# A fused LayerNorm, S5 state space and GLU kernel: the first block set by hand, weight pair 0 on two DMA rings ahead of x tiles 2 and 3

## The chip, the core and the metric

The kernel runs on one core of a Trainium2 chip. The metric is the device time of one execution in microseconds (us); medians are over several executions, and before and after were run in turn on the same chip. An execution counts as slow when it is more than 1.5% above the fastest of its kernel.

Below, TensorE is PE in the profile, its weight loads PEld, VectorE DVE, ScalarE ACT, GpSimd POOL, SyncE SP. Times in traces are from the start of the core's span, which is about 1.8 us shorter than the device time. A profiled run is one execution, so its details can differ from the median's.

## The reference

```python
xn = layernorm(x)                       # x: 2048 tokens of 576
h[t] = Lam_bar * h[t-1] + B_bar @ xn[t] # 576 complex states
y = 2 * real(C @ h) + xn * Dskip
g, u = xn @ w_gate, xn @ w_up           # 576 to 4608
out = x + y + (sigmoid(g) * u) @ w_down # 4608 to 576, bf16 out
```

Most of the time is in the three large products of the last line. The tokens are worked in blocks of 512 (four tiles of 128), two blocks at a time, and the 4608 hidden columns in 36 chunks of 128. For TensorE the kernel transposes the normalised x: xT holds, for a block, the 576 features over partitions.

## The kernel before, as far as the argument goes

The kernel writes the work of all engines in one order, and a queue of background work (`bg`) is dealt out to DVE and ScalarE between groups of matmuls. Loads, in program order (in the trace of the kernel before, what SyncE issues moves on queue q1, 29808 packets, and what ScalarE issues on q10, 432 packets, both listed as hardware; GpSimd's is on q0, 12672 packets, listed as software; a ring is such a queue below):

```python
for tt in range(TT_B):                          # x tiles 0..3, 144 KB each, rows of 1152 bytes
    load_x(tt, nc.sync if tt % 2 == 0 else nc.scalar)
for pr in range(2):                             # weight pairs 0, 1: 576 KB each, rows of 512 bytes
    load_wgu((0, pr), nc.gpsimd, nc.gpsimd)
for tt in range(TT_B, 2 * TT_B):                # x tiles 4..7 (block 1)
    load_x(tt, nc.gpsimd, "hst")
for pr in range(2, 4):
    load_wgu((0, pr), nc.gpsimd, nc.gpsimd)
# ... Dskip
load_wgu((0, 4), nc.gpsimd, nc.gpsimd)
```

A weight pair holds the gate and up columns of two chunks. One gate/up group is 18 matmuls of 64 rows and 512 columns. Groups 0 and 1 are begun by hand on the first two tiles while tiles 2 and 3 are still being normalised; then come groups 2 to 9 of block 0, and then groups of block 1, whose xT comes by four DMA transposes that SyncE issues:

```python
busy(10, TB); busy(6, P)                        # dummy matmuls
for tt in range(2):
    ln_stats(tt); ln_std(0, tt, tt + 1)
for tt in range(2):
    ln_recip(0, tt, tt + 1); ln_norm(tt, twice=False)
    start_transpose(tt)                         # TensorE
busy(20, P)
start_copy(0, slice(0, NH), nc.scalar.copy)     # PSUM to xT
ln_stats(2)
start_copy(1, slice(0, 5), nc.scalar.copy)
# ... statistics of tile 3, rest of copy 1 on DVE, norms of tiles 2 and 3
start_groups[0].mms(slice(0, 2 * P))            # 18 matmuls of 256 columns
start_transpose(2); start_transpose(3)
start_groups[1].mms(slice(0, 2 * P))
# ... copies of tiles 2 and 3
for g in start_groups:
    g.mms(slice(2 * P, TB))
for tt in range(TT_B, 2 * TT_B):                # block 1's LayerNorm: background work
    bg.add(1.05, lambda tt=tt: ln_stats(tt))
# ... std, norms, ln_dma_transpose(4..7), 8 residuals, then
bg.add(1.0, exp_first, ready=lambda: consts_at[0] is not None and consts_at[0] + 4 <= bg.now)
```

`exp_first` makes tables for the state space part from nine small constant loads (`load_consts`), which are issued among the groups of block 1.

Of the kernel before, what the change touches and what calls it, by code (L numbers as in the profile page):

```python
# [66 lines left out]
def kernel(  # L67
# [65 lines left out]

    def load_x(tt, eng, tag=None):
        if tag is None:
            xt = lnp.tile([P, D], BF16, name="xt", bufs=8)
        else:
            xt = hpool.tile([P, D], BF16, name="xt0", tag=tag, bufs=10)
        eng.dma_start(xt[:], x[tt * P:(tt + 1) * P, :])
        xts[tt] = xt  # L140
# [23 lines left out]
    make_identity(nc, ident[:])  # L164
    for tt in range(TT_B):
        load_x(tt, nc.sync if tt % 2 == 0 else nc.scalar)
    for pr in range(2):
        load_wgu((0, pr), nc.gpsimd, nc.gpsimd)
    for tt in range(TT_B, 2 * TT_B):
        load_x(tt, nc.gpsimd, "hst")  # L170
    for pr in range(2, 4):
        load_wgu((0, pr), nc.gpsimd, nc.gpsimd)
    dskip_rows = consts.tile([P, D], BF16, name="dskip_rows")
    nc.gpsimd.dma_start(dskip_rows[:], A_Dskip.partition_broadcast(P))
    load_wgu((0, 4), nc.gpsimd, nc.gpsimd)

# [12 lines left out]
    ldt = consts.tile([P, NU], FP32, name="ldt")  # L189
    consts_at = [None]  # L190

    def load_consts():
        for (dst, src) in ((ldt, A_log_dt), (lre, A_Lambda_re), (lim, A_Lambda_im)):
            nc.gpsimd.dma_start(dst[:, 0:PT], src[0:R0].rearrange("(a p) -> p a", p=P))
            for h0 in (0, H):
                nc.gpsimd.dma_start(dst[h0:h0 + H, PT:NU], src[R0:NS].rearrange("(a b) -> a b", b=1))
        consts_at[0] = bg.now

# [284 lines left out]
    class GateUp:  # L483
# [5 lines left out]

        def mms(self, cols=slice(0, TB)):  # L490
            w = wgu_t[(self.slot, self.f // FP)]
            fs = slice((self.f % FP) * P, (self.f % FP + 1) * P)
            for c in range(NH):
                for gi, rows in ((0, slice(0, H)), (1, slice(H, P))):
                    nc.tensor.matmul(self.ps[:, gi, cols], w[rows, c, fs], xT[self.nb][rows, c, cols],  # L495
                                     start=c == 0, stop=c == NH - 1)
# [65 lines left out]
    def d_step(tt, terms, final, last=False):  # L562
# [8 lines left out]
        if last:  # L571
            ob = lnp.tile([P, D], BF16, name="ob", bufs=2)
            for a, eng in ((0, nc.sync), (1, nc.scalar)):
                cs = slice(a * DH, (a + 1) * DH)
                pd = ps_pair("pd")
                for i in range(n):
                    mm(pd[:, 0, 0:DH], i, a)
                nc.vector.tensor_add(ob[:, cs], acc[:, cs], pd[:, 0, 0:DH])
                eng.dma_start(o[tt * P:(tt + 1) * P, cs], ob[:, cs])
# [154 lines left out]

    busy(10, TB)
    busy(6, P)

# [5 lines left out]
    def start_copy(tt, cs, eng):  # L743
        eng(xT_tile(0)[:, cs, tt * P:(tt + 1) * P], ptrs[tt % 2][:, cs, :])  # L744

    for tt in range(2):
        ln_stats(tt)
        ln_std(0, tt, tt + 1)
    for tt in range(2):
        ln_recip(0, tt, tt + 1)  # L750
        ln_norm(tt, twice=False)
        start_transpose(tt)
    busy(20, P)
    start_copy(0, slice(0, NH), nc.scalar.copy)
    ln_stats(2)
    start_copy(1, slice(0, 5), nc.scalar.copy)
    ln_std(0, 2, 3)
    ln_stats(3)
    ln_std(0, 3, 4)
    start_copy(1, slice(5, NH), nc.vector.tensor_copy)  # L760
    for tt in range(2, TT_B):
        ln_recip(0, tt, tt + 1)
        ln_norm(tt, twice=False)
    start_groups[0].mms(slice(0, 2 * P))
    start_transpose(2)
    start_transpose(3)
    start_groups[1].mms(slice(0, 2 * P))
    for tt in range(2, TT_B):
        start_copy(tt, slice(0, 5), nc.scalar.copy)
        start_copy(tt, slice(5, NH), nc.vector.tensor_copy)  # L770
    for g in start_groups:
        g.mms(slice(2 * P, TB))
    for tt in range(TT_B, 2 * TT_B):
        bg.add(1.05, lambda tt=tt: ln_stats(tt))
    bg.gap()
    bg.add(0.0, lambda: ln_std(1, 0, TT_B))
    bg.add(0.2, lambda: ln_recip(1, 0, TT_B))
    for tt in range(TT_B, 2 * TT_B):
        bg.add(0.9, lambda tt=tt: ln_norm(tt))
        bg.add(0.0, lambda tt=tt: ln_dma_transpose(tt))  # L780
    bg.add(0.0, lambda: ln_done.add(1))
    bg.add(0.0, bg.owe)
    for tt in range(0, 2 * TT_B):
        bg.add(1.25, lambda tt=tt: ln_resid(tt))
    bg.gap()
    bg.add(1.0, exp_first, ready=lambda: consts_at[0] is not None and consts_at[0] + 4 <= bg.now)
    bg.gap()
    bg.add(1.5, angles_small)
    for pt in range(NU):
        for which in range(2):  # L790
            bg.add(1.35, lambda pt=pt, which=which: angle(pt, which))
    bg.step(3.2)
    for g in start_groups:
        g.evac()
        used(g)
        bg.step(4.5)

# [4 lines left out]
    for sb in range(NSB):  # L802
        b0 = sb * NB_SB
        for c in range(NC):
# [15 lines left out]
            if slot == 0:  # L820
                run_groups([GateUp(slot, f, nb) for (f, nb) in order[:8]])
                catch_up_ln(1)
                order = order[8:]
                side_loads.extend([load_consts] + bt_loads)
            run_groups([GateUp(slot, f, nb) for (f, nb) in order])
# [63 lines left out]
```

## Time and profile before

| | before |
|---|---|
| device time, median of the 3 executions | 508.96 us (508.66 to 509.38) |
| span of the profiled execution | 506.5 us |
| first 512-column matmul (group 2) | 13.65 us |
| x tiles 2 and 3 landed | 4.43 and 4.26 us |
| last weight piece of pair 4 landed; fourth DMA transpose of block 1 | 21.62; 27.53 us |
| the 640 ns step at the wait on hT | 59.06 us |
| start of the last 42 matmuls | 497.45 us |

TensorE is busy from the first group to the end (500.9 of 506.5 us, 99%). (It takes 13.87 us for the first 512-column matmul; counting again gives 13.65, and that figure is used from here on.) One view that it does not show is SyncE's own, where the issue of the four transposes stands:

```profile
17.60 7.33 SPq L260 DMA_TRANSPOSE xT<-xn  x4
```

Start, length, what: SyncE needs 7.3 us to issue four transposes of block 1, beginning when the first norm is ready.

### The profile page before, as it was taken

What the parts mean: (1) busy time and instruction counts of PE and PEld (TensorE: products, weight loads), DVE (VectorE), ACT (ScalarE), POOL (GpSimd) and SP (SyncE); (2) the same over time, 40 slices, a digit from 0 to 9 for tenths busy, and PEclk for the clock granted to TensorE, in tenths of its full rate; (3) what the DMA queues carried; (4) which work ended last, traced back from release to release, by engine and by line L of the source; (5) the groups of instructions that cost most, each with busy time, mean ns of one, the idle gap of its engine ahead of it and who ended that gap; (6) DMA issues with size and microseconds to landing.
All of it is one profiled execution on the core that took longest, in us unless ns stands there. A gap on an engine that the chain in (4) does not pass through costs nothing.

```text
span 506.5 us, 10662 instructions
## 1 busy us (share of the span) xinstructions
PE 500.9 (99%) x4536; PEld 290.1 (57%) x4536; DVE 324.1 (64%) x703; ACT 204.9 (40%) x368; POOL 96.9 (19%) x143
## 2 busy tenths in 40 slices
PE   8999999999999999999999999999999999999997
PEld 6444575444477444477754444774444774446775
DVE  6964999886888797868878767786765222221111
ACT  4767623556500756520035655006555005553000
POOL 7138420123100043110001231000431001300000
PEclk9999999999999999999999999999999999999999
DMA  8999895246220099261430652200753201600001
GB/s 211 206 181 163 204 188 98 55 110 141 49 48 25 1 145 199 58 149 37 89 77 11 155 132 55 49 25 1 160 114 79 48 25 39 171 1 4 33 25 36
DMA packets 42959, 45.59 MB, mean 90 GB/s; under 512 B 30496, under 2 KB 34336, under 8 KB 42912
## 3 DMA queue, kind: packets, MB, share of 16 engines
q0 software_dynamic: 12672, 34.23, 31.1%
q1 hardware_dynamic: 29808, 10.33, 10.7%
q8 instruction: 35, 0.57, 0.5%
q10 hardware_dynamic: 432, 0.37, 0.2%
q14 instruction: 12, 0.10, 0.1%
HBM read 34.36 MB, written 2.36 MB: 72 GB/s over the span
## 4 chain that ended last, share of the span: by engine, by line
PE 94%; DVE 3%; ACT 1%; DMA 1%; issue 0%
PE pgu L495 52%; PE pd L569 34%; PE pbu L524 7%; DVE sctab L325 1%; DVE rnd L324 1%; DMA xt<-in_A_x_dram 1%; DVE ang L349 1%; PE ptr L741 0%; DVE hT L504 0%; ACT xT L744 0%; DVE bnst L224 0%; ACT L328 0%; ACT uT L502 0%; ACT L501 0%; ACT sT L501 0%
## 5 line engine op out<-in xcount | busy, mean ns | idle before, releaser
L495 PE MATMUL pgu<-xT,wgu 64*128 64x512 bf16 (+1 forms) x2628 | 283.7, 373 | 0.0
L495 PEld LDWEIGHTS <-wgu 64*128 64x128 bf16 x2628 | 127.6, 94 | 151.1 <-issue 0.5
L569 PE MATMUL pd<-wd,hT 128*128 128x288 bf16 x1152 | 144.8, 286 | 0.4 <-DVE hT L504 0.4
L501 ACT ACTIVATE sT<-pgu 128x512 bf16<-128x512 f32 x144 | 86.4, 600 | 120.4 <-PE pgu L495 110.3
L569 PEld LDWEIGHTS <-hT 128*128 128x128 bf16 x1152 | 112.1, 98 | 31.3 <-DVE hT L504 1.5
L504 DVE TENSOR_TENSOR hT<-sT,uT 128x512 bf16<-128x512 bf16 x144 | 60.7, 423 | 100.3 <-ACT uT L502 100.1
L502 ACT CAST uT<-pgu 128x512 bf16<-128x512 f32 x144 | 83.9, 583 | 0.0
L154 POOL DMA_DIRECT2D wgu<-in_B_w_gate_dram x36 | 27.9, 776 | 227.2 <-PE pgu L495 208.2
L160 POOL DMA_DIRECT2D wd<-in_B_w_down_dram x36 | 26.6, 755 | 100.2 <-PE pd L569 100.2
L530 ACT COPY bure<-pbu 128x512 f32<-128x512 f32 x16 | 9.4, 588 | 87.8 <-PE pbu L524 75.4
L589 DVE TENSOR_TENSOR acc<-acc,pd 128x576 f32<-128x576 f32 x32 | 24.1, 752 | 24.5 <-PE pd L569 24.5
L586 DVE TENSOR_TENSOR ob<-acc,pd 128x576 bf16<-128x576 f32 x15 | 11.3, 754 | 38.0 <-PE pd L569 38.0
L524 PE MATMUL pbu<-xT,bt 64*128 64x512 bf16 x288 | 33.7, 376 | 0.0
L569 PEld LDWEIGHTS <-hst 128*128 128x128 bf16 x288 | 28.2, 98 | 7.1
L154 POOL DMA_DIRECT2D wgu<-in_B_w_up_dram x36 | 26.8, 745 | 2.7 <-DMA wgu<-in_B_w_up_dram 1.9
L569 PE MATMUL pd<-ctre,hst 128*128 128x288 bf16 x128 | 26.5, 286 | 0.0
L569 PE MATMUL pd<-ctim,hst 128*128 128x288 bf16 x128 | 26.5, 286 | 0.0
L439 DVE TENSOR_TENSOR_SCAN gre<-r,g0re,wrim 128x512 bf16<-128x512 f32 x20 | 25.6, 1279 | 0.0
L524 PEld LDWEIGHTS <-bt 64*128 64x128 bf16 x288 | 13.7, 94 | 17.1 <-issue 0.7
L446 DVE TENSOR_TENSOR_SCAN gim<-r,g0im,wrim 128x512 bf16<-128x512 f32 x16 | 20.4, 1275 | 0.0
L224 DVE BATCH_NORM_STATS2 bnst<-xt 128x6 f32<-128x288 bf16 x32 | 12.6, 435 | 2.2 <-DMA xt<-in_A_x_dram 2.2
L501 ACT ACT_TABLE_LOAD x6 | 7.7, 1283 | 15.5 <-PE pgu L495 15.4
(113 smaller groups left out, 280.8 us busy)
## 6 DMA issues: line engine op xcount, KB each, us to landing
wgu<-in_B_w_gate_dram POOLq DMA_DIRECT2D x36, 288.0 KB, 4.4
wgu<-in_B_w_up_dram POOLq DMA_DIRECT2D x36, 288.0 KB, 5.2
wd<-in_B_w_down_dram POOLq DMA_DIRECT2D x36, 288.0 KB, 6.1
out_dram<-ob SPq DMA_DIRECT2D x15, 144.0 KB, 1.8
xt<-in_A_x_dram SPq DMA_DIRECT2D x10, 144.0 KB, 2.8
xt<-in_A_x_dram POOLq DMA_DIRECT2D x4, 144.0 KB, 6.6
bt<-ctre POOLq DMA_DIRECT2D x2, 288.0 KB, 7.2
bt<-ctim POOLq DMA_DIRECT2D x2, 288.0 KB, 8.0
```

The costliest lines, as they stand in the source:

```text
L154: eng.dma_start(w[rows, :, :], src[:, fs].rearrange("(c p) f -> p c f", p=H))
L160: nc.gpsimd.dma_start(wd[:], B_w_down[f0:f0 + FP * P, :].rearrange("(n p) d -> p n d", p=P))
L224: nc.vector.bn_stats(st[:, gi, :], xt[:, gi * DH:(gi + 1) * DH])
L439: nc.vector.tensor_tensor_scan(gre[:], r_bc, w[:, 0, :], g0re[:, col], ALU.mult, ALU.add)
L446: nc.vector.tensor_tensor_scan(gim[:], r_bc, w[:, 1, :], g0im[:, col], ALU.mult, ALU.add)
L495: nc.tensor.matmul(self.ps[:, gi, cols], w[rows, c, fs], xT[self.nb][rows, c, cols], start=c == 0, stop=c == NH - 1)
L501: nc.scalar.activation(sT[:], self.ps[:, 0, :], ACT.Sigmoid)
L502: nc.scalar.copy(uT[:], self.ps[:, 1, :])
L504: nc.vector.tensor_mul(h[:], sT[:], uT[:])
L524: nc.tensor.matmul(out, w, xT[self.nb][rows, c, ts_], start=c == 0, stop=c == NH - 1)
L569: nc.tensor.matmul(out, lhsT, rhs[:, a * DH:(a + 1) * DH], start=i == 0, stop=i == n - 1)
L589: nc.vector.tensor_add(halves(acc[:]), halves(acc[:]), pd[:, :, 0:DH])
```

## The change

The intent: let the real matmuls start earlier, with fewer instructions between. Weight pair 0 no longer queues on GpSimd, but goes first on the two hardware rings, behind x tiles 0 and 1 and ahead of 2 and 3. The rest of the loads are held back: a tiny DVE memset on x tile 4 makes GpSimd's ring wait until DVE has done tiles 0 and 1. The matmuls of the start go tile by tile in 128 columns, block 1's LayerNorm is written in place and not in the background, the constants are loaded right behind weight pair 4, and the last tile is split 448 + 128 and not 288 + 288.

```diff
-    for tt in range(TT_B):
-        load_x(tt, nc.sync if tt % 2 == 0 else nc.scalar)
-    for pr in range(2):
-        load_wgu((0, pr), nc.gpsimd, nc.gpsimd)
...
+    for tt, eng in ((0, nc.sync), (1, nc.scalar)):
+        load_x(tt, eng)
+    load_wgu((0, 0), nc.sync, nc.scalar)
+    for tt, eng in ((2, nc.sync), (3, nc.scalar)):
+        load_x(tt, eng)
+    def load_behind():
+        for tt in range(TT_B, 2 * TT_B):
+            load_x(tt, nc.gpsimd, "hst", held=tt == TT_B)   # held: memset of xt[:, 0:2] on DVE
+            if tt == TT_B + 1:
+                load_wgu((0, 1), nc.gpsimd, nc.gpsimd)
+        ...                                                 # pairs 2, 3, Dskip, pair 4
+        load_consts()
...
-    busy(10, TB)
-    busy(6, P)
+    busy(11, TB)
...
+    load_behind()                    # after ln_stats and ln_std of tiles 0 and 1
...
-    busy(20, P)
+    busy(1, TB)
...                                   # all copies of tiles 0 and 1 on ScalarE
+    for cs in (range(0, 5), range(5, NH)):
+        for g in range(2):
+            start_mms(g, 0, cs)
     for tt in range(2, TT_B):
         ln_recip(0, tt, tt + 1)
         ln_norm(tt, twice=False)
+        start_transpose(tt)
+        start_mms(tt - 2, 1)
+        start_copy(tt, CA, nc.scalar.copy)
...
+    for tt in range(2, TT_B):
+        start_mms(0, tt)
+    start_groups[1].mms(slice(2 * P, TB))
...                                   # stats, norms and DMA transposes of tiles 4..7 in place
-    bg.add(1.0, exp_first, ready=lambda: consts_at[0] is not None and consts_at[0] + 4 <= bg.now)
+    bg.add(1.0, exp_first)
...
-            for a, eng in ((0, nc.sync), (1, nc.scalar)):
+            for eng, cs in ((nc.sync, slice(0, D - P)), (nc.scalar, slice(D - P, D))):
```

## The prediction

> **What bounds the kernel now.** I read the busy shares first, then TensorE's waits, then the chain that ended last in order of time, cut to the first 60 us.
>
> ```profile
> PE 500.9 (99%) x4536; PEld 290.1 (57%) x4536; DVE 324.1 (64%) x703; ACT 204.9 (40%) x368; POOL 96.9 (19%) x143
> ```
>
> TensorE is busy for 99% of a 506.5 us span. A busy TensorE can still be stretched, so I measured the starts of its matmuls in the trace: 107.9 ns from one 64-row, 512-column matmul to the next (18 make a gate/up group, 1.94 us), and 122.7 ns for one of 288 columns. From the first 512-column matmul at 13.87 us on, that sums to 142 groups x 1.94 + 16 state groups x 1.94 + 4 x 0.98 + 1440 x 0.1227 = 487.6 us, and 13.87 + 487.6 = 501.5, against a last matmul that starts at 502.47. So the middle is solid, and only what lies before 13.87, after 502.5, and one us between can be won. The waits of TensorE say the same:
>
> ```profile
> PE pgu L733 <- DVE warm L182: 1.3, 1, 1.3
> PE pd L569 <- DVE hT L504: 0.4, 1, 0.4
> PE ptr L741 <- DVE xn L249: 0.3, 1, 0.3
> ```
>
> The reader should see only one wait in the body, 0.4 us (the second row). In starts it is one step of 640 ns where 123 is usual, so 0.52 us lost, at 59.1 us. The chain shows the two ends of that, and the start:
>
> ```profile
> 0.74 2.67 DMA xt<-in_A_x_dram
> 3.44 0.83 DVE bnst L224 x2
> 4.29 0.21 DVE mv L225
> 4.50 0.69 DVE bnst L224 x2
> 5.22 0.21 DVE mv L225
> 5.49 0.44 DVE xn L249
> 5.98 0.71 PE ptr L741 x18
> 6.71 1.72 ACT xT L744 x2
> 8.48 1.16 PE pgu L495 x18
> 9.63 1.12 PE ptr L741 x36
> 10.76 30.27 PE pgu L495 x306
> ...
> 58.09 0.51 DVE rnd L324
> 58.62 0.69 DVE sctab L325
> 59.31 0.34 DVE hT L504
> 59.70 0.30 PE pd L569
> ```
>
> Columns are start, length, what. Start: load x, LayerNorm on DVE, transposes on TensorE, then 1.72 us of ScalarE copies during which TensorE runs 20 dummies. At 59.3 us the product hT comes late because DVE has been working through angle tables back to back since 48.3 us.
>
> [...] dummy matmuls of 512 columns start 427 ns apart until 4.64 us and faster after, and 128-column ones 56 ns apart. [...] both hardware rings together moved the first x tiles at about 370 KB per us, and later the engines are full while POOL's weights alone move at about 200 KB per us. [...] Before, weights and transposes do overlap at 19 us. [...]
>
> **The change, part by part.**
>
> *Dummies.* 10 of 512 and 6 of 128 become 11 of 512; that ends at about 5.4 us, before the first transpose (5.98). The 20 dummies become one. Nothing on the path[...].
>
> *Weight pair 0.* Before, its halves land at 6.62 and 7.88 us (landings in the trace). Now they follow x tiles 0 and 1 on two hardware rings. Those two (288 KB, 370 KB per us from about 1.7 us) have moved by 2.6[...]. The pair is 576 KB in rows of 512 bytes: at 200 to 275 KB per us 2.1 to 2.9 us, so it lands at 5.5 to 6.3. Enough in either case. x tiles 2 and 3 come after it: 288 KB more, 0.8 us, landing 6.2 to 7.0 (before: 4.26 and 4.43). DVE is ready for tile 2 at 6.45, so this is where the change may cost.
>
> *Copies and the first matmuls.* ScalarE copies 5 of 9 blocks (0.65 us, from the copies of 640 columns) instead of 9. Matmuls may start at 7.5 instead of 8.48. They are 36 of 128 columns, at 56 ns a pair ([...]the dummies' pitch) 1.0 us: done at about 8.55.
>
> *Tile 2.* DVE: two statistics and aggregates for tiles 2 and 3 (1.98 us, as before from 6.38 to 8.36), reciprocal, norm: transposes at 6.6 + 2.65 = 9.27 (before 9.57). The DVE copy that stood between is now on ScalarE. Then TensorE: transposes 0.53, group 0 on tile 1 0.50, transposes 0.53, then 0.50 x 3 and 0.98, plus 0.5 for four switches of kind (0.15 to 0.2 each before, where some overlap): 4.55. The first 512-column matmul starts at 9.27 + 4.55 = 13.82, against 13.87. The gain of the early start is lost again as idle time from 8.55 to 9.27. **Start: 0.0**, from -0.15 (x2 landed in time) to +0.7 (landed 7.2, with ScalarE held up by its issues).
>
> *LN of block 1 in place.* Statistics of tiles 4 to 7 start when tile 3's copy leaves DVE, about 12.9, and end at 15.7; two products, square root (two table loads of 1.28), norms at about 17.3 instead of 16.7. The four DMA transposes landed 23.4 to 27.5 before; the ninth group after the start needs them at 13.8 + 8 x 1.94 = 29.4. Later norms: 28.1. But the nine small constant loads now queue just behind weight pair 4, at about 22 us, not at 35 to 42: some 1,920 packets of 22 ns each, over 16 engines 2.6 us[...]. Worst case 28.1 + 2.6 = 30.7, a wait of 1.3 us; best case none. **I count +0.2.**
>
> *Constants early.* exp comes after evacuation 13 instead of 16, so the angle tables start on DVE near 40 us, not 48.3. Nine sets of 1.54 plus nine products of 0.36 end near 57.3, and the last product is bound by its own inputs (ready near 57.7), ahead of its use at 59.1. **-0.5.** The program order of the two DVE streams confirms that the sets now begin after product 13 and not 16.
>
> *Last tile.* 288 + 288 columns become 448 + 128: 21 x (189 + 56) = 5.15 us, before 42 x 122.7 = 5.15. The last add shrinks from 0.46 us (288 columns) to about 0.30, since 576 columns take 0.75 and so one column 1.0 ns:
>
> ```profile
> 502.79 0.46 DVE L578 TENSOR_TENSOR ob<-acc,pd 128x288 bf16<-128x288 f32 x1 [2.12 <-PE pd L569]
> 503.28 0.35 ACTq L579 DMA_DIRECT2D out_dram<-ob  x1
> ```
>
> [...] **-0.15.**
>
> Sum: 0.0 + 0.2 - 0.5 - 0.15 = -0.45, so 508.96 - 0.45 = 508.5.
>
> **Rivals.** *A real gain at the start* (1 us): the matmuls do start 1 us earlier, and if x tile 2 landed by 6.4 and nothing else queued, steady work would start near 13.7; even then my sum gives only -0.15 there, so 508.3. For it to be 1 us, statistics and norms of tiles 2 and 3 would have to run faster than the trace's durations. *Weight transfer turned into a new wait*: 1,152 rows of 512 bytes on the hardware rings move slower than I think, or hold up ScalarE's first square root behind its issues. Each 0.1 us of lateness of tile 2 goes straight into the end; 0.7 gives 509.2. *Block 1 comes late*: transposes against constants, up to +1.3, giving 509.6. *The clock falls back* for lack of dummies[...].
>
> **Range and chances.** The bad cases are +0.7 and +1.1 over my mid values, unlikely together; the good case is -0.35. Run to run the kernel spreads 0.7. That gives 507.5 to 509.6. A change of 2% is 10 us, twenty times anything in the sum, so faster 0.015, slower 0.015.
>
> **What would show it.** First gate/up matmul near 7.5 (right) or after 8 (weights late). A TensorE gap ahead of tile 2's transposes, ended by DVE, of about 0.7. First 512-column matmul at 13.7 to 14.2. No wait on hT near 59 us. A wait of TensorE on a DMA transpose of xT near 29.4 would show the constants in the way. The last add at 0.30 us. The prediction would be wrong if the fast clock were lost, if tile 2 landed after 7.3, or if a product's lateness moved to another stage.

Passages that no trace of this case shows are cut from the prediction, each cut marked. The landing times of pair 0 and of tiles 2 and 3 contain 0.8 us from the last data to the landing, an estimate (the four x tiles of the kernel before landed 0.5 to 0.6 us after theirs); that the fast clock would stay was assumed; that the constants delay the transposes, in the +0.2, was assumed too, the 2.6 us being their packets' own time; and the reason given for the time behind the last add was not what the trace shows (before, the last store landed 1.63 us after its issue, at 504.91, and the span ended 1.61 us later).

What the trace of the kernel before has: dummies of 512 columns 427 ns apart until 4.64 us, then one step of 370 and one of 216, and 56 ns between those of 128; 376 and 385 GB/s in the two halves of the us from 2.5, with 4% or less of the engines' time on GpSimd's ring; 215 GB/s at a share of 0.97 from 4 to 8 us; from 18 to 20 us 0.34 MB on GpSimd's ring and 0.11 MB on SyncE's, which are the transposes; 371 packets of the constants from 39 to 40 us at a share of 0.491, so 21 ns each.

## The result, and the profile after

The changed kernel took **511.12 us** in the median of 6 executions (510.03 to 518.92; the highest is a slow one), the kernel before 509.11 in 6 of the same rounds (508.66 to 509.53, all fast). The five fast executions of the changed kernel have a median of 510.55; one of them, the longest (512.61), had a clock of 0.995. The ratio of times is 1.0038, with a 95% interval of 1.0018 to 1.0058. Ratios are computed as the mean time of one kernel's fast runs over that of the other's of the same rounds, so they are not quite the ratio of the medians quoted. The interval excludes 1, and the median lies 1.5 us above the top of the predicted range, that of the fast executions 0.9 us. The prediction was wrong. The profiled executions (508.32 and 510.03 us) are the fastest of each kernel.

The page of the changed kernel shows 30 more matmuls and a busy TensorE as before:

```profile
PE 501.4 (99%) x4566; PEld 292.1 (57%) x4566; DVE 324.0 (64%) x703; ACT 205.9 (41%) x370; POOL 95.7 (19%) x141
```

TensorE's waits (line, what it waited for: us in total, times, longest) have changed place:

```profile
PE ptr L748 <- DVE xn L257: 1.5, 1, 1.5
...
PE pgu L503 <- issue: 0.4, 1, 0.4
```

The wait on hT is gone. In its place TensorE waits 1.5 us ahead of tile 2's transposes, and 0.4 us for something to which the view gives only the word "issue". The chain that ended last, in order of time, shows where that comes from:

```profile
2.00 6.27 DMA xt<-in_A_x_dram
...
8.29 0.83 DVE bnst L232 x2
...
10.82 0.69 PE ptr L748 x18
...
12.75 4.14 PE pgu L503 x85
16.89 0.07 issue
16.96 14.40 PE pgu L503 x131
31.36 0.36 issue
31.71 27.37 PE pgu L503 x252
```

Read from the top: x tile 2 took 6.27 us from its issue at 2.00 to its landing at 8.27. DVE, idle from 6.6, then did the statistics of two tiles and one norm, and TensorE transposed tile 2 at 10.82 and not at 9.56. There are two breaks behind that: 16.89, where nothing in the profile is waited for, and 31.36. At the second, the trace has an instruction of TensorE's sequencer that waits for the second and fourth transposes of block 1; it ended at 31.66, and the fourth had landed at 31.62. (The matmul also waits for ScalarE, whose last work before it had ended at 30.53.) SyncE began to issue them 2 us later than before:

```profile
19.61 8.17 SPq L268 DMA_TRANSPOSE xT<-xn  x4
```

The tail: in the timeline the last add is shorter by 0.17 us (it was 0.46).

```profile
504.80 0.29 DVE L586 TENSOR_TENSOR ob<-acc,pd 128x128 bf16<-128x128 f32 x1 [0.55 <-PE pd L585]
```

So the two profiled executions differ by these terms, taken from the starts of the matmuls. The 64-row matmuls run in pairs, 216 ns from pair to pair, the two of a pair up to 20 ns apart; the step at the break stands within a pair and is counted whole:

| place | before | after | difference |
|---|---|---|---|
| first 512-column matmul | 13.65 | 15.22 | +1.57 |
| break near 17 us (a step of 441 ns) | none | 0.44 | +0.44 |
| wait ahead of block 1 (a step of 732 ns, 215 expected) | none | 0.52 | +0.52 |
| wait on hT at 59 us | 0.52 | none | -0.52 |
| start of the last 42 matmuls | 497.45 | 499.46 | **+2.01**, the sum |
| from there to the end | 9.07 | 8.80 | -0.27 |
| span | 506.52 | 508.26 | **+1.74** |

Why x tile 2 landed so late is to be seen in the windows (stretch; its length; busy us of PE, PEld, DVE, ACT and POOL with instruction counts; granted clock; busy share of the DMA engines; GB/s). Before:

```profile
3.00:4.00 1.00, 1.00 (x4) 0.39 (x3) 0.56 (x2) 0.00 (x0) 1.00 (x3) 1.00 1.20 337
8.00:10.00 2.00, 1.95 (x42) 1.66 (x41) 1.75 (x7) 0.80 (x3) 1.28 (x2) 1.00 1.09 235
```

After:

```profile
3.00:4.00 1.00, 1.00 (x4) 0.38 (x3) 0.50 (x2) 0.89 (x1) 0.00 (x0) 1.00 0.67 180
8.00:10.00 2.00, 1.18 (x36) 1.01 (x36) 1.68 (x5) 1.00 (x3) 2.00 (x4) 1.00 0.67 186
```

Before, two x tiles and the weights of GpSimd's ring fill the engines together: a share of 1.20 and 337 GB/s. After, GpSimd's ring is held (its first load is issued at 5.82 us), and in the fourth us only one ring carries data, ScalarE's (q10; q1 is SyncE's), in rows of 512 bytes:

```profile
q10 hardware_dynamic: 343, 0.18, 66.3%
q1 hardware_dynamic: 5, 0.00, 0.8%
```

(packets, MB, share of the engines, from 3 to 4 us). SyncE had issued its half of the pair at 1.19 us, but its data begins only at about 4.0; why is not shown, but the traces of after_again, a_merged and a_consts_late have nearly the same hole (5 to 15 KB on q1 in that us). From 4 to 6 us both rings run together, at 233 GB/s and a share of 1.03. The share falls to 0.67 once more at 8 to 10 us, when the hardware rings are done and GpSimd's ring, two x tiles of block 1 behind it, only begins with its weights. Summed over the first 10 us, 1745 KB have arrived and not 2009.

### The profile page after: what moved, and what is told of

It is laid out like the page before. It is cut to its first block, busy times and chain, and to the rows that moved or that the text cites. A ratio compares the mean times of both kernels' runs of the same rounds, so it can differ in the third digit from the quotient of the medians.

```text
span 508.3 us, 10728 instructions
## 1 busy us (share of the span) xinstructions
PE 501.4 (99%) x4566; PEld 292.1 (57%) x4566; DVE 324.0 (64%) x703; ACT 205.9 (41%) x370; POOL 95.7 (19%) x141
## 4 chain that ended last, share of the span: by engine, by line
PE 97%; DMA 1%; DVE 1%; SPq 0%; issue 0%
PE pgu L503 55%; PE pd L577 34%; PE pbu L532 7%; DMA xt<-in_A_x_dram 1%; PE pd L585 1%; DVE bnst L232 0%; PE ptr L748 0%; SPq L157 0%; DVE xn L257 0%; DVE mv L233 0%; SPq L142 0%; DVE ob L586 0%; DVE rstd L240 0%
## 5 line engine op out<-in xcount | busy, mean ns | idle before, releaser
L503 PEld LDWEIGHTS <-wgu 64*128 64x128 bf16 x2682 | 131.1, 94 | 149.0 <-issue 1.8
L577 PE MATMUL pd<-wd,hT 128*128 128x288 bf16 x1128 | 141.4, 286 | 0.0
L577 PEld LDWEIGHTS <-hT 128*128 128x128 bf16 x1128 | 109.9, 98 | 30.1 <-issue 0.8
L577 PEld LDWEIGHTS <-hst 128*128 128x128 bf16 x270 | 26.4, 98 | 6.7
L577 PE MATMUL pd<-ctre,hst 128*128 128x288 bf16 x120 | 24.5, 286 | 0.0
L577 PE MATMUL pd<-ctim,hst 128*128 128x288 bf16 x120 | 24.5, 286 | 0.0
```

The lines of the kernel that those rows point to most:

```text
L503: nc.tensor.matmul(self.ps[:, gi, cols], w[rows, c, fs], xT[self.nb][rows, c, cols], start=c == 0, stop=c == NH - 1)
L577: nc.tensor.matmul(out, lhsT, rhs[:, a * DH:(a + 1) * DH], start=i == 0, stop=i == n - 1)
```

## The experiments

My theory had three parts. (1) *x tiles 2 and 3 late*: the whole start is late because they wait behind a slow weight pair. (2) *Instruction fetch*: the break near 17 us is TensorE waiting for its own instructions. (3) *Block 1's transposes*: the wait at 31 us is on the DMA transposes, held up by the constants, as the prediction had it; the rival is that they wait for the weight stream, which now ends later. Twelve kernels ran (a_no_w4b under the label a_no_w4 first, which no chip ran). The table has what their traces show; "break" is the step to the next matmul when the trace holds 449 instructions of TensorE (447 matmuls and weight loads, and two of its sequencer at the start), a place that comes back below; where it is 0, the step is the usual one. Times (us) are of the one profiled execution; only the last column is of all fast ones.

| kernel | first 512-column matmul | break | weight pair 4 landed | 4th transpose landed | block 1 begins | median of the fast executions (ratio to before, 95%) |
|---|---|---|---|---|---|---|
| before | 13.65 | 0 | 21.62 | 27.53 | 29.19 | 509.11, in after's rounds |
| after | 15.22 | 0.44 | 24.80 | 31.62 | 31.71 | 510.55 (1.0038: 1.0018 to 1.0058) |
| after_again | 15.39 | 0 | 24.75 | 31.85 | 31.94 | 510.73 (1.0032: 1.0016 to 1.0048) |
| a_x_first | 13.35 | 0.52 | 24.55 | 31.40 | 31.49 | 509.76 (1.0007: 0.9992 to 1.0022) |
| a_w0_pool | 13.53 | 0 | 25.06 | 31.73 | 31.87 | 510.49 (1.0025: 0.9997 to 1.0052) |
| a_unheld | 19.85 | 1.62 | 25.05 | 33.10 | 36.81 | 514.52, two, clock 0.993 (1.0105: 1.0086 to 1.0124) |
| a_merged | 15.73 | 0 | 24.78 | 31.08 | 31.27 | 509.93 (1.0015: 0.9999 to 1.0032) |
| a_dummies20 | 15.40 | 0 | 25.19 | 31.75 | 31.84 | 510.39 (1.0020: 1.0005 to 1.0035) |
| b_split | 16.81 | 3.12 | 22.83 | 29.29 | 32.35 | 513.18 (1.0074: 1.0040 to 1.0107) |
| a_consts_late | 15.10 | 0.85 | 24.89 | 31.51 | 31.60 | 511.00 (1.0032: 1.0017 to 1.0047) |
| b_consts_tail | 13.81 | 0 | 23.74 | 30.50 | 30.64 | 510.04 (1.0014: 0.9989 to 1.0038) |
| a_no_w4b | 13.47 | 0 | not loaded | 29.78 | 29.87 | 508.18, two |
| best_a | 13.90 | 0.73 | 24.21 | 30.65 | 30.79 | 508.32 (0.9981: 0.9967 to 0.9995) |
| best_b | 13.91 | 0 | 22.55 | 28.30 | 29.45 | 515.92, clock 0.993 (1.0134: 1.0118 to 1.0150) |

Names that begin with a_ are edits of the kernel after, those with b_ of the kernel before; best_a is an edit of after, best_b of before.

### The change once more (after_again)

No edit.

> The changed kernel once more, for a second trace beside the variants. If the readings so far are of the kernel and not of one execution: x tiles 2 and 3 land near 8.1 us, the first 512-column matmul starts at 15.1 to 15.5, TensorE stands without a semaphore at its instruction 449 for 0.3 us or more (unless the packet ends before about 15.1), the fourth DMA transpose lands 6 to 7 us after weight pair 4, after 31, and TensorE waits on it 0.2 us or more; time 0.3 to 0.6% over the kernel before. If they are of one execution, at least one of these is gone.

511.05 us, 1.0032: the result repeats (510.73 in the three fast executions). The trace repeats the late tile (landings 8.22 and 8.44, first 512-column matmul at 15.39), but not the break near 17 us; the wait ahead of block 1 is 0.98 and not 0.52, and block 1 begins at 31.94 against 31.71. So the break is of single executions, and where it fails to come, the wait ahead of block 1 grows in its stead: block 1 begins when its transposes have landed, 0.09 us after the fourth in both traces. (Of this run's expectations, the break is the one that clearly failed.)

### The order of the first loads (a_x_first, a_w0_pool, a_unheld)

```diff
 # a_x_first                                      # a_w0_pool
-    load_wgu((0, 0), nc.sync, nc.scalar)         -    load_wgu((0, 0), nc.sync, nc.scalar)
     for tt, eng in ((2, nc.sync), (3, nc.scalar)):    # the same
         load_x(tt, eng)
+    load_wgu((0, 0), nc.sync, nc.scalar)         +    load_wgu((0, 0), nc.gpsimd, nc.gpsimd)
 # a_unheld
-            load_x(tt, nc.gpsimd, "hst", held=tt == TT_B)
+            load_x(tt, nc.gpsimd, "hst")
     # and load_behind() is called ahead of the LayerNorm of tiles 0 and 1
```

> The changed kernel with one thing undone: x tiles 2 and 3 are issued ahead of weight pair 0 on the same two hardware rings. Theory 'order' (the weights ahead of tiles 2 and 3 made the start late): tiles 2 and 3 land near 4.3 us as before instead of 8.05 and 8.27, the transposes of tile 2 begin near 9.5 instead of 10.82, the first 512-column matmul near 13.9 instead of 15.22, and the time falls by 1.0 to 1.5 us against the changed kernel. The first gate/up matmul then waits for the weights, near 8.5. Rival 'the ScalarE copies or DVE set the start': tile 2's transposes stay within 0.3 us of 10.8 though the tiles land early.

> The changed kernel with weight pair 0 issued by POOL at the start as before the change, and x tiles 0 to 3 alone on the two hardware rings. Theory 'order and idle DMA engines' (the start is late because tiles 2 and 3 follow 512-byte rows on the hardware rings, and block 1 is late because POOL's stream of weights starts at 7 us and not at 3 us): tiles 2 and 3 land near 4.3 us, the first 512-column matmul starts near 13.4, weight pair 4 lands near 22 instead of 24.8, the fourth DMA transpose near 28 instead of 31.6, and TensorE waits on it under 0.4 us. A stall with no semaphore at TensorE instruction 449 of 0.3 us or more remains. Time 1.5 to 2.5 us under the changed kernel. Rival 'the LN of block 1 in place is too slow by itself': the fourth transpose still lands after 30 and TensorE waits 1 us.

> The changed kernel with the hold on POOL's stream removed (no write into tile 4, the loads behind it issue from 1.5 us on). Theory 'idle DMA engines': the engines are full from 2 us on, weight pair 4 lands near 23 instead of 24.8 and the fourth DMA transpose near 29.5 instead of 31.6; but weight pair 0 and tiles 2 and 3 now share the engines, tiles 2 and 3 land after 9.5, the first 512-column matmul starts after 16.5, and TensorE no longer waits on the fourth transpose. Time within 0.8 us of the changed kernel, since one late thing is traded for another. Rival 'the hold costs nothing': pair 4 and the fourth transpose land as late as before.

With the tiles ahead of the weights they land by 5.4 us, tile 2's transposes start at 8.96 and the first 512-column matmul at 13.35, which is 1.87 us earlier than after. That shows part 1: the lateness of the start is the order of the loads. The weight pair itself is not later for it (7.34 and 7.76 us, against 7.22 and 8.08). But in this trace almost nothing of the 1.87 us arrives at block 1. TensorE's waits in a_x_first:

```profile
PE pgu L503 <- ACT uT L510: 1.1, 1, 1.1
...
PE pgu L503 <- DMA wgu<-in_B_w_up_dram: 0.6, 1, 0.6
```

The second row is weight pair 2, which landed at 18.50; the matmul lost 0.77 us in starts. The first is the wait ahead of block 1, 1.28 us lost. The view names ScalarE's copy, which ended at 31.49; the fourth transpose landed at 31.40, and TensorE's sequencer waited for it until 31.44. Both ended within 0.1 us, so this trace alone could not tell them apart. Block 1 begins at 31.49, only 0.22 us earlier than in the profile of the kernel after. In the medians of the fast executions a_x_first is 0.8 to 1.0 us faster than the changed kernel (509.76 against 510.55 and 510.73; by the ratios to before it is 0.25 to 0.31%, 1.3 to 1.6 us), and level with the kernel before. They ran in different sessions, and the intervals of these ratios are 0.15 to 0.2% to each side, so the size is rough. It is more than the trace shows, and less than 1.87: the profile of after was the fastest of its executions, 0.5 us under the median of the fast ones, and where the others lost that is not recorded. So the order of the loads is worth about 1 us in the time, and the rest of what it gives at the start is taken by the next waits.

a_w0_pool says the same more plainly, because there the chain names the transposes itself:

```profile
18.39 7.96 PE pgu L503 x71
...
26.48 5.25 DMA xT<-xn
31.73 0.14 issue
31.87 4.26 PE pgu L503 x37
```

TensorE waits for pair 2 until 18.34, and for the transpose until 31.73: 1.81 us lost in that wait. So only the start was as expected for this run: pair 4 was to land near 22 and the fourth transpose near 28, with a wait under 0.4, a break was to remain (there was none), and the time was to fall by 1.5 us or more (it was 510.49). By its signs the rival named there came true, that block 1's LayerNorm in place is too slow by itself; a_no_w4b below speaks against it. In the DMA windows of this kernel, where GpSimd's ring carries pair 0 from the start but is still held behind it, the early stretch is full (327 GB/s from 3 to 4 us) and a hole comes at 6 to 8 us:

```profile
6.00:8.00 2.00, 1.71 (x38) 1.25 (x38) 1.93 (x8) 1.08 (x3) 2.00 (x4) 1.00 0.55 138
```

Taking the hold away (a_unheld) was no remedy, and pair 4 (25.05) and the transposes (33.10) came no earlier, as the rival had it. x tiles 4 and 5 and pair 1 then move at the same time as pair 0, which lands at 8.46 and 9.55, tiles 2 and 3 at 9.83 and 11.57, and the first 512-column matmul starts at 19.85. With the hold these loads landed earlier (7.22 and 8.08, 8.05 and 8.27). The profiled execution is one of the two slow ones (523.14 us); the start lies long before the slowness begins, which is a wait of 6.66 us at 212.5 us for a DMA transpose of a later block, after which pairs of matmuls start 427 ns apart for some 3 us. All four executions had a clock of 0.993 or less, so the size of its loss is not compared further.

### The break near 17 us (a_merged, a_dummies20, b_split)

The trace lists the transfers of the instruction queue. In the kernel after one was in flight from 14.14 to 15.56 us, and TensorE went on at 16.96; it stopped with 449 instructions begun. If that is a block of instructions not yet there, the place must stay the same when other instructions stand around it.

```diff
 # a_merged
-    for tt in range(2, TT_B):
-        start_mms(0, tt)
-    start_groups[1].mms(slice(2 * P, TB))
+    for g in start_groups:
+        g.mms(slice(2 * P, TB))                     # 18 matmuls fewer
 # a_dummies20
+    for i in range(20):                             # ahead of tile 2's transposes, where TensorE idles
+        nc.tensor.matmul(start_groups[0].ps[:, i % 2, 3 * P:TB], warm[:, 0:P], warm[:, 0:P], start=True, stop=True)
 # b_split (the kernel before)
-    start_groups[0].mms(slice(0, 2 * P))
+    for tt in range(2):
+        start_groups[0].mms(slice(tt * P, (tt + 1) * P))
     # and so for the other three calls: 72 matmuls more, no other change
```

> The changed kernel with tiles 2 and 3 of group 0 in 18 matmuls of 256 columns instead of 36 of 128 (18 fewer matmuls, 36 fewer TensorE instructions). Theory 'instruction fetch': the stall at 16.5 us (0.44 us) is gone or under 0.1, for about 0.1 us of later start since the matmuls of tile 2 wait for tile 3's copy; time -0.2 to -0.4 us. Rival 'hiccup': the stall stays at the same time of the run, and the time is the same or 0.1 worse.

> The changed kernel with 20 dummy matmuls of 128 columns (40 TensorE instructions, 1.1 us) put into the idle 1.7 us ahead of tile 2's transposes, where they cost no time by themselves. Theory 'instruction fetch' (the stall of 0.44 us at 16.5 us, which waits for no semaphore, is TensorE at the end of its instructions, until the first 16 KB block of the run has come): 40 instructions more bring the end of the instructions forward by 20 matmuls of 108 ns, about 2.1 us, while the block comes at most 1 us earlier, so the stall moves to about 14.5 to 15.5 us and grows to 1 us or more; the time grows by 0.5 to 2 us. Rival 'a one-off hiccup of memory or clock': no stall or the same one, and the time is unchanged. A third reading, that the missing dummies let TensorE's clock fall back, would make this run faster and its granted clock 1.000 in every timed run.

> The kernel before with one thing added: the four sets of 18 start matmuls of 256 columns are 36 of 128 columns each, the same array time with 72 matmuls and 144 TensorE instructions more. Theory 'instruction fetch' (in three traces TensorE stood without a semaphore wait at exactly its 449th instruction, until about 1.4 us after a 16 KB instruction packet had ended): TensorE reaches its 449th instruction near 13 us instead of 18 us, and the block is there at 15 to 17 us, so it stands still there for 2 to 4 us and the time grows by 1.5 to 4 us. Rival 'not the fetch': no stall at that instruction, start of the 512-column matmuls near 13.8, time within 0.4 us of the kernel before.

b_split speaks clearest. It is the kernel before with its loads untouched and matmuls of 128 columns in place of 256, and it stands still for almost 3 us (its timeline of TensorE: start, length, what; in brackets the idle time and its releaser):

```profile
10.70 2.40 PE L495 MATMUL pgu<-xT,wgu 64*128 64x128 bf16 x79
16.01 4.23 PE L495 MATMUL pgu<-xT,wgu 64*128 64x128 bf16 x59 [2.91 <-issue]
```

It stops behind its 449th instruction and goes on with the 450th, exactly as the kernel after did, though the time is another. (Its median overstates the break: three of its four executions, all counted fast, had a clock of 0.996 or 0.997; the profiled one, at 1.000, took 511.59 us.) Here are all traces in which the step at that place was lengthened, with the transfer on the instruction queue ahead of it (us):

```
kernel          stops   goes on  step   transfer on the instruction queue
after           16.52   16.96    0.44   14.14 to 15.56
a_x_first       14.65   15.17    0.52   12.68 to 13.78
a_consts_late   16.39   17.24    0.85   14.12 to 15.53
a_unheld        21.14   22.77    1.62   19.76 to 21.17
b_split         12.89   16.01    3.12   13.07 to 14.46
best_a          17.13   17.86    0.73   15.11 to 16.54
```

TensorE goes on 1.3 to 1.7 us after the end of the transfer, every time at the same instruction; in b_split the transfer even began after TensorE had stopped. The other eight traces fit the same lag: there TensorE came to this place 1.46 us or more after the end of the transfer (after_again: end at 15.23, place at 16.69), and did not stop. The trace doesn't name the engine for which a transfer is, so I go by the counts: over a whole run this queue (q8) carries 35 blocks of 16384 bytes in before and in after, one for every 259 and 261 TensorE matmuls and weight loads in the mean (9072 and 9132), while the next busiest engine, DVE, has 703 instructions in all. So I read the break as TensorE's fetch of its instructions; behind the first of these blocks the only steps over 330 ns in these two traces are the wait ahead of block 1 and the wait on hT. In a_merged, where 18 matmuls fewer stand ahead of that place, TensorE came to it only at 18.8, after a transfer that ended at 16.34, and the step is not lengthened. a_dummies20 was a miss on my part: 20 more matmuls ahead should have brought the place forward and made the break longer, and there was none. Its transfer came earlier as well (11.96 to 13.42), while TensorE had done 272 instructions; in all the other traces it had done 348 to 449. So small instructions ahead of the break cost only in the traces in which TensorE came to its 449th instruction less than 1 us after the end of the transfer, or before it (0.96 us in after, 1.57 us before it in b_split). What starts a fetch is not shown by these traces.

The 18 matmuls fewer of a_merged may be worth something in the medians (509.93 against 510.55 and 510.73 in the fast executions), though in its trace the first 512-column matmul starts at 15.73, 0.5 us later than after, because one larger piece waits for the copy of tile 3. Its block 1 begins at 31.27, 0.19 us after its transposes landed.

### Block 1 and the constants (a_consts_late, b_consts_tail, a_no_w4b)

```diff
 # a_consts_late: constants as in the kernel before
-        load_consts()                               # behind weight pair 4
-    bg.add(1.0, exp_first)
+    bg.add(1.0, exp_first, ready=lambda: consts_at[0] is not None and consts_at[0] + 4 <= bg.now)
-                side_loads.extend(bt_loads)
+                side_loads.extend([load_consts] + bt_loads)
 # b_consts_tail: the kernel before with the reverse of this, and with the 448 + 128 tail
 # a_no_w4b: a_x_first; the tile of pair 4 is set to zero on DVE, and not loaded (a wrong result on purpose)
         if key == (0, 4):
             w = consts.tile([P, NH, FP * P], BF16, name="wgu4", tag="T1")
+            nc.vector.memset(w[:], 0.0)
+            wgu_t[key] = w
+            return
-        load_wgu((0, 4), nc.gpsimd, nc.gpsimd)
```

> The changed kernel with the nine constant loads back where they were (behind the first groups, needed 4 groups later). Theory 'constants in the way': the fourth DMA transpose of block 1 lands near 29 instead of 31.62 and the 0.52 us wait of TensorE on it near 31 us is gone; and the wait on the product hT near 59 us (0.52 before the change, none after) comes back. Rival 'late norms alone': the fourth transpose still lands after 31 and TensorE still waits 0.3 us or more. Time: near zero net under the first theory, up to +0.5 under the second.

> The kernel before with only the two parts of the change that the trace shows to gain: the constant loads right behind weight pair 4 (and no gate on their landing for exp), and the last tile split 448 and 128. Theory 'the two small gains stand alone': the 0.52 us wait on hT near 59 us is gone, the end after the last step is 0.27 us shorter, and the fourth DMA transpose still lands before 29.2, so the time is 0.5 to 0.9 us under the kernel before. Rival 'constants delay the transposes here too': the fourth transpose lands after 29.5, and TensorE waits for it, which gives the gain back.

> The kernel a_x_first with one thing taken out: weight pair 4 (576 KB) isn't loaded; its tile is set to zero on DVE in the first 3 us, so the results of two of the 36 hidden chunks, groups 8 and 9, are wrong on purpose. In a_x_first that pair landed at about 25, the four DMA transposes of block 1 were issued from 18.5 us on and the fourth landed at 31.4, and TensorE waited 1.28 us at 30.0. Theory A (the transposes hardly advance until the weight stream has ended, and land 5.7 to 7.1 us after its last piece): the last piece is now weight pair 3, at 21.5 or so, the fourth transpose lands at 27.2 to 28.6, the wait near 30 is gone, the ninth group after the start begins near 30.2 instead of 31.49, and the time is 1.0 to 1.3 us under that of a_x_first: 508.3 to 508.8. The wait for weight pair 2 near 17.5 stays at 0.6 to 0.9. Rival B (the transposes are limited by SyncE's own issuing of them, 9.5 us for four, or by the time at which the norms are ready): the issue times stay, the fourth still lands at 31 or later, the wait and the time of a_x_first (509.8) stay.

The constants are not the main cause. With them out of the way (a_consts_late) the fourth transpose landed at 31.51 against 31.62, and block 1 began at 31.60. What came back is the wait on hT, a step of 791 ns at 61.49. So the prediction had put the gain of the early constants right and their price wrong: block 1 begins as late without them. A few tenths are not excluded: with the constants right behind pair 4 the fourth transpose landed 6.3 to 7.1 us after it, without them 5.7 to 6.6 (a_unheld and a_no_w4b left out).

The traces have one thing in common. In 13 of the 14 the first transpose of block 1 landed 0.9 to 2.0 us after the last weight piece of the first stream, wherever between 17.6 and 19.8 us SyncE had begun to issue it (in a_unheld it was issued too late for that, at 24.26). By that piece's landing 117 to 204 KB of the four transposes' 1180 KB had moved. The fourth landed 5.7 to 7.1 us after weight pair 4 in the 12 traces that loaded it in time: 5.9 before, 6.8 after, 6.6 with the constants taken away from after. In the five traces with the load order of before (before, b_split, b_consts_tail, best_a, best_b), pair 4 landed at 21.6 to 24.2, 23.0 in the mean; in the five with that of after (after, after_again, a_merged, a_dummies20, a_consts_late) at 24.75 to 25.19, 24.9 in the mean. The weights end 1.9 us later, and with them the transposes. One doubt stays: the latest of the first five is best_a, with 24.21, and it alone of them has block 1's LayerNorm in place. So the in-place work may have a part in the late end of the weights; no run separates the two.

a_no_w4b tests whether the transposes follow the weights, by taking 576 KB out of the stream. The last weights landed at 21.01, the first transpose 2.0 us after them at 23.00, the fourth at 29.78 where a_x_first had 31.40, and the wait ahead of block 1 is down to 0.17 us:

```profile
18.03 16.33 PE L506 MATMUL pgu<-xT,wgu 64*128 64x512 bf16 x147 [0.30 <-DMA wgu<-in_B_w_up_dram]
```

One stretch from 18.03 on, in which the view finds no break at 30 (in starts, a step of 386 ns where 215 is usual). Block 1 begins at 29.87 against 31.49, 1.62 us earlier, and the two fast executions, 508.11 and 508.24 us, are 1.5 to 1.7 us under a_x_first's median. The rival, that SyncE's issuing or the norms alone set the time, would have kept 31. But my figure of 27.2 to 28.6 for the fourth landing was too early: it is 8.8 us after the last weights, not 5.7 to 7.1. With the weights gone, two things are left in this trace: SyncE's own issuing (7.83 us from 18.11, and the fourth was issued only at 23.77; four transposes took 6.4 to 9.6 us to issue in the nine traces in which I looked), and the constants, landing until 26.87. Which of them held the fourth is not shown. Two of its four executions were slow (516 us); nothing in the fast trace says why.

b_consts_tail shows the other side of the early constants. In the order of before they bring nothing: the time is 1.0014 of before's (the interval includes 1), not the gain of 0.8 us that the terms of the wait on hT and the tail would give. Block 1 waits 1.28 us for transposes landing at 30.50. That is 6.8 us after this trace's own late pair 4 (23.74), so it doesn't show that the constants held them up. Then TensorE loses 1.02 us more:

```profile
30.80 0.21 ACT L328 ACTIVATE dt<-ldt 128x5 f32<-128x5 f32 x1
32.91 0.21 ACT L330 ACTIVATE r<-r 128x5 f32<-128x5 f32 x1 [1.91 <-DVE r L329]
33.14 1.28 ACT L501 ACT_TABLE_LOAD   x1
```

ScalarE sits between the two exponentials of `exp_first` for 1.91 us, until DVE has made the product that the second one reads, then loads the sigmoid's table, and only then empties the next group; TensorE waited for that (its waits name ScalarE's copy, 0.9 us).

### Two kernels put together from this (best_b, best_a)

best_b is the kernel before with the new tail and with the constants in between: issued behind a DVE memset after five of the eight residuals, so that they can't come among the transposes. best_a is the hand-made start and tail of the change, but with the loads in the order of before, 18 matmuls fewer in the start, and the constants held behind four residuals.

```diff
 # both: the constants' loads wait for DVE
+    def held_consts():
+        for t in (ldt, lre, lim):
+            nc.vector.memset(t[:], 0.0)
+        load_consts()
         bg.add(1.25, lambda tt=tt: ln_resid(tt))
+        if tt == TT_B - 1:                          # TT_B in best_b
+            bg.add(0.2, held_consts)
 # best_a: loads as before; and in the start
         start_transpose(tt)
-        start_mms(tt - 2, 1)
+        if tt == 2:
+            start_mms(0, 1)
...
-    for tt in range(2, TT_B):
-        start_mms(0, tt)
-    start_groups[1].mms(slice(2 * P, TB))
+    start_groups[1].mms(slice(P, 3 * P))
+    start_groups[0].mms(slice(2 * P, TB))
+    start_mms(1, 3)
```

> The kernel before with the tail of the change and the constants held until five residual tiles are done, so behind the DMA transposes. Theory 'the constants delayed the transposes when they came right behind pair 4': the fourth transpose lands under 29.5 again instead of 30.5, the wait near 29 us (1.28 in the run with early constants) falls under 0.4, the wait on hT near 59 stays away, the end is 0.27 shorter: 0.4 to 0.9 us under the kernel before. Rival: the fourth transpose lands after 30 all the same, and the time is above the kernel before.

> A version built from the findings: the loads in the order of the kernel before (tiles 0 to 3 on the hardware rings, all weights on POOL from the start), the hand-made first block of the change with 18 fewer matmuls and tile 4's statistics behind the copies, the constants held until four residual tiles are done, the tail 448 and 128. If the causes are right: transposes of tile 2 near 9.0, first 512-column matmul at 13.3 to 13.8, no stall at instruction 449, weight pair 4 near 22.5, fourth transpose near 29 and TensorE's wait for it under 0.4 us, no wait on hT near 59: 0.3 to 1.0 us under the kernel before. If block 1 comes late for another reason, TensorE waits 1 us near 29 and the time is that of the kernel before or worse.

best_b failed, and it shows how. Its transposes landed at 28.30, in time. But the first exponential stands in ScalarE's program at 34 us and the constants land between 31.71 and 37.88:

```profile
34.08 1.28 ACT L331 ACT_TABLE_LOAD   x1 [4.97 <-DMA ldt<-in_A_log_dt_dram]
```

ScalarE idles 4.97 us for them, the evacuations stand behind it, and TensorE waits:

```profile
PE pgu L498 <- ACT uT L505: 6.3, 1, 6.3
```

After that wait, pairs of matmuls start 427 ns apart until 42.7 us, the pitch of the very first dummies, and all four executions have a mean clock of 0.993.

best_a worked: **508.32 us** (507.94 to 509.26, 5 executions), ratio 0.9981 (0.9967 to 0.9995), the only kernel whose interval lies below 1, with a correct result. Its waits:

```profile
PE pgu L502 <- DMA xT<-xn: 0.5, 1, 0.5
PE pgu L502 <- issue: 0.4, 1, 0.4
```

The break behind instruction 449 and the wait ahead of block 1 are both still there, 0.73 and 0.63 us in starts, against the expectation (no break, a fourth transpose near 29, a wait under 0.4); the wait on hT is gone and the tail is shorter, and these two terms alone are some 0.8 us. Its gain over the kernel before, about 1 us of 509, was measured in one session of five rounds.

## Why the prediction was wrong

*What bounds the kernel.* Right: the body is TensorE's, and the difference came from the start, from waits, and from the tail. The sum over those places meets the difference of the two profiled spans.

*Weight pair 0 and tiles 2 and 3, the step that failed.* The prediction gave the pair 5.5 to 6.3 us and the tiles "landing 6.2 to 7.0", at 200 to 275 KB per us, and with that a start term of 0.0, at worst +0.7. The pair landed at 7.22 and 8.08, the tiles at 8.05 and 8.27, and the term was **+1.57**. The rate for the pair was not what failed: while both rings ran, from 4 to 6 us, 233 GB/s came. What failed is the overlap. The first two tiles' 288 KB had arrived only by 3.0 us, not by 2.6; then SyncE's ring stood empty for 1 us (180 GB/s in the fourth us, at a share of 0.67); and the two tiles behind the pair did not come in 0.8 us. The prediction's 864 KB in 2.8 to 3.6 us are 246 to 316 GB/s; from 3 to 7 us it was 205. The prediction's own sign of error, tile 2 after 7.3, came true. The rule of the rival, that each 0.1 us of lateness of tile 2 goes straight into the end, held for the start; a_x_first shows that undoing the order gives 1.87 us back there.

*Copies and the first matmuls.* Predicted from 7.5; they began at 8.12, because the weights came last (8.08), not the copies. A gap of 0.7 us ahead of tile 2's transposes was expected and was 1.5. The tile-2 work from there to the first 512-column matmul took 4.40 us (10.82 to 15.22), predicted 4.55.

*Instruction fetch.* Not in the prediction at all, neither as a step nor as a rival: **+0.44** in the profiled execution, 0 in the second, steps of 0.5 to 3.1 in five other kernels. What was needed stood in the trace of the kernel before: an instruction queue, q8, with 35 blocks of 16384 bytes, one for some 260 TensorE instructions. No such step shows in that trace, and in the one after only at the first block (0.44 us); b_split, with 3.1 us there, had the largest. That the step is this fetch is my reading of the counts and of the lag.

*Block 1.* The prediction counted +0.2 (0 to 1.3) and blamed the constants ("transposes against constants"). It measured **+0.52** in this execution, 0.98 in the next, and the constants were not what set it (31.51 without, 31.62 with). What was missed is that the weight stream would end later, at 24.8 and not 21.6, and the transposes with it. The norms came later than predicted too (18.7 against 17.3; 16.7 before), but the first transpose then still landed only after the weights. The prediction had seen weights and transposes overlap at 19 us, and took it that transposes would advance beside the weights; in these traces the first landed only 0.9 to 2.0 us after the last weights, when 117 to 204 KB of the four's 1180 KB had moved. Either half of the new load order went with the late end: a_w0_pool has only the hold (25.06), a_unheld only the weights on the hardware rings (25.05); both have the LayerNorm in place. Why both come to the same time is open. So is how much of the 3.2 us between the two profiles is the change's, since in the order of before the landing varied from 21.6 to 24.2; the first profile was a lucky one (the earliest of the five), and my need of 29.4 against a landing of 27.5 looked safer than it was.

*Constants early.* -0.5 predicted, **-0.52** measured, and a_consts_late brings it back. Right, by the mechanism named.

*Tail.* -0.15 predicted, **-0.27** measured. The add went from 0.46 to 0.29 as worked out; the rest is in the store, which I had held equal: 1.63 us from its issue to its landing before, 1.52 after.

*The rivals.* "Weight transfer turned into a new wait" was the right one, and its 0.7 was half of what came. "The clock falls back" did not happen: the mean granted clock of the profiled execution was 1.0. (The pitch of the first matmuls did halve later there, at 6.9 us and not at 4.9: pairs of 128-column transposes were 104 ns apart until 6.94 us and 53 to 54 after it, where before the step of 427 ns between 512-column dummies gave way to 216 by 5.23. It was without cost: the first group waited for its weights until 8.1.) "A real gain at the start" needed tile 2 by 6.4; a_x_first and a_w0_pool gave it that, were 1.7 to 1.9 us ahead of the change at the first 512-column matmul, and were within 0.3 us of it where block 1 begins, because of the waits for pair 2 and for block 1. The range was too narrow on the upper side: it took the bad cases as independent and small. The late tile, the late block 1 and the late instructions are all waits for transfers, which the page counts on the same 16 DMA engines; that they come together for this reason is my reading, which no run tests.

## What to carry to other kernels

When loads are put in another order, work out when the last one of the stream ends and what queues behind it, not only whether the first need is met: here a gain of 1.87 us at the start was worth about 1 us, since the next waits, for transfers on full DMA engines (a share of 1.02 to 1.06 from 10 to 17 us after), took the rest. A rate read from a full stretch did not hold here where a ring stood empty (337 GB/s at a share of 1.20 with three rings before, 180 at 0.67 with one after): look for such stretches. And before small instructions are put where TensorE is fast, look at the transfers of its instruction queue too: in 6 of 14 traces TensorE stopped behind its 449th instruction, in steps of 0.44 to 3.12 us, until 1.3 to 1.7 us after one of them.
